# A convolution with top-1 mixture of experts on one core: the list rows of a routing unit made as an outer product of 16-bit one-hots

## The chip, the cores and the metric

The program runs on one core of a Trainium2 chip. Its metric is the device time of one execution in microseconds (us); the kernel before takes 1145.64 us, the median of three runs from 1144.6 to 1146.14 us. Engines are named as in the profile: PE multiplies matrices, PEld is its loading of weights, DVE, ACT and POOL are the vector, scalar and general engines, SP issues transfers.

## The reference

A short causal convolution comes first. Each of 8 heads has 7 taps, made into weights by a softmax; head h of token s is the weighted sum of the same 24 columns of tokens s-6 to s.

```python
x_pad = np.concatenate([np.zeros((B, pad, D)), x], axis=1)      # B 8, S 2880, D 192
x_unf = x_pad[:, idx, :].reshape(B, S, K, H, group)
x = np.einsum('hk,bskhg->bshg', w, x_unf).reshape(B * S, D)     # 23040 tokens
```

Then each token goes to one of 4 groups (largest logit of x @ w_group), and in it to one of 4 experts (largest logit of x @ w_expert[g]). Its output is the product of the two softmax values times relu(x @ w1[g, e]) @ w2[g, e], with 1024 hidden features.

```python
mask_e = e_idx == e
h = np.maximum(xg[mask_e] @ w1[g, e], 0.0)
out[tok_idx] = combined[:, None] * (h @ w2[g, e])
```

So every token needs its row, its scale, and a place in the list of its expert; the list tells the expert stage which rows to fetch.

## The kernel before

**Units.** Routing is cut into 192 blocks of 120 tokens, and these into 18 units u0 to u17: of 4, 8, 12, 8, 8 and 8 blocks, and then of 12 each. `unit(u)` (L402) is a generator that yields between its steps, so that a unit's steps are issued between those of its neighbours and, later, between the steps of the experts. A unit loads x, runs the convolution on PE (L452) and copies it on ACT into a tile xc (L461; three buffers), transposes it (L475, L483), takes the logits (L495, L497, L500), turns them back (L507, L508) and decides on DVE (L539 to L568). L568 writes the scale into xc, and L570 stores xc to a table xcd in device memory, from ACT's queue. A later unit's L461 takes the buffer again, and so waits for that store to land.

**The list rows.** ohx (bf16, block innermost) is the one-hot of the 16 experts; L557 sums it over the blocks into cum. L579 and L580 are two small matmuls on the last column of cum; from them come the running ends of the lists and the place of each token (L583 to L591). L593 and L595 split a place into one of 128 rows of its window (16 experts, 8 eighths each) and one of 32 columns. Then, in halves of `HB2` = 6 blocks, L608 compares a table of 128 numbers with the row (ohl, f16, 128 numbers a block), L615 compares a table of 32 with the column (ohr), and L619 multiplies ohr by the token's number (ohv). From u6 on (`LP`) these stand in the written order, with yields between (`HGAP`, `LG`). L624 to L626 make rowi, the table rows that the unit writes. L633 multiplies ohl by ohv, one matmul of 128 weights a block, summed over the unit's blocks: 192 in all, with 192 moving columns (the 32, six times) in u0 to u7 and 32 in the others. L640 and L642 turn the sum into token numbers (lsi), and the POOL issues a transfer (L645) that writes lsi into the table idtab.

**The table's fill.** Before any of that, two transfers (L269, L272, `clear_table`) fill idtab from SBUF. Their source, `fill`, takes a buffer of the tile ohl (L265), which has two in the pool.

**Experts.** From unit u5 on (`NEED`) the expert stage runs beside routing: lists are loaded (L1157), rows gathered (L717), turned (L750 to L767), the hidden layer is computed (L817 or L786), then back (L835, L839 or L801, L805), L898 scales the result into ys, and L888 scatters it. Loads of expert weights (L666 to L670) go through SP's queue, and DVE and ACT cast them (L683, L691, L698).

The order of each engine is fixed when the program is built: the generators say what may come next, and a planner merges the steps by their costs.

## Time and profile before

| | |
|---|---|
| median of three runs | 1145.64 us (1144.6 to 1146.14) |
| the profiled execution | 1152.26 us |
| its span, first to last instruction | 1150.4 us |
| granted clock of PE, mean | 0.977 |
| PE busy | 1072.8 us, 93% |
| PEld busy | 971.1 us, 84% |
| DVE busy | 752.4 us, 65% |
| ACT busy | 644.1 us, 56% |
| POOL busy | 523.5 us, 46% |

The first expert matmul starts 117.87 us after the first instruction; the last of the lists is written at about 445 us. Rows of the trace are in microseconds from the span's start. What stands in square brackets in a row is the time for which that engine sat idle just before, and what ended the idle time. The busy share of the whole span is a mean over stages that have different limits.

### The profile page before, as it was taken

What the parts mean: (1) busy time and instruction counts of PE and PEld (TensorE: products, weight loads), DVE (VectorE), ACT (ScalarE), POOL (GpSimd) and SP (SyncE); (2) the same over time, 40 slices, a digit from 0 to 9 for tenths busy, and PEclk for the clock granted to TensorE, in tenths of its full rate; (3) what the DMA queues carried; (4) which work ended last, traced back from release to release, by engine and by line L of the source; (5) the groups of instructions that cost most, each with busy time, mean ns of one, the idle gap of its engine ahead of it and who ended that gap; (6) DMA issues with size and microseconds to landing.
All of it is one profiled execution on the core that took longest, in us unless ns stands there. A gap on an engine that the chain in (4) does not pass through costs nothing.

```text
span 1150.4 us, 20931 instructions
## 1 busy us (share of the span) xinstructions
PE 1072.8 (93%) x7124; PEld 971.1 (84%) x7124; DVE 752.4 (65%) x1671; ACT 644.1 (56%) x1362; POOL 523.5 (46%) x611
## 2 busy tenths in 40 slices
PE   6565999998999998999999999999999999999996
PEld 4444788987989998889899999999999988989986
DVE  3465878987778756576565555655556665687874
ACT  5445657765657554454455445554545555677873
POOL 3004143333334454554545454545445554487773
PEclk9878989999999999999999999999999999999998
DMA  8767688999566432332253223322333435499970
GB/s 185 186 158 228 160 222 215 252 234 216 156 155 164 122 106 85 116 112 67 83 137 113 72 76 99 113 74 73 103 101 106 133 92 157 116 257 257 252 201 19
DMA packets 143167, 166.08 MB, mean 144 GB/s; under 512 B 18946, under 2 KB 124397, under 8 KB 143054
## 3 DMA queue, kind: packets, MB, share of 16 engines
q1 hardware_dynamic: 100974, 111.04, 36.4%
q0 software_dynamic: 18752, 35.85, 10.5%
q10 hardware_dynamic: 23328, 17.80, 6.6%
q8 instruction: 57, 0.93, 0.3%
q14 instruction: 56, 0.46, 0.1%
HBM read 129.43 MB, written 36.58 MB: 144 GB/s over the span
## 4 chain that ended last, share of the span: by engine, by line
PE 70%; DMA 5%; DVE 5%; issue 4%; ACT 3%; POOL 1%; POOLq 0%; ACTq 0%; DVEq 0%
PE ph L786 21%; PE ph L817 11%; PE pm L801 7%; PE po L801 7%; PE po L835 7%; PE pm L805 3%; PE po L805 3%; PE po L839 3%; PE pm L452 3%; DMA rawc<-in_moe_w 2%; DMA xg<-xcd,idpt 2%; DVE hl L823 1%; DVE cw L698 1%; PE ph L852 1%; PE ph L750 1%
## 5 line engine op out<-in xcount | busy, mean ns | idle before, releaser
L888 POOL DMA_INDIRECT out<-ys,idp x160 | 174.3, 1090 | 267.9 <-DVE ys L898 192.0
L791 DVE SCALAR_TENSOR_TENSOR hl<-ph,hh 128x512 fp32r<-128x512 f32 x208 | 142.2, 689 | 141.7 <-ACT hh L790 141.3
L790 ACT ACTIVATE hh<-ph 128x512 fp32r<-128x512 f32 x208 | 123.0, 600 | 170.6 <-PE ph L786 167.6
L717 POOL DMA_INDIRECT xg<-xcd,idp x160 | 175.3, 1096 | 93.8 <-issue 40.5
L835 PE MATMUL po<-cw,hh 128*128 128x384 f32 x592 | 193.2, 379 | 3.0 <-DVE ys L898 3.0
L817 PE MATMUL ph<-xa,ah 128*128 128x256 f32 x592 | 169.2, 307 | 0.0
L839 PE MATMUL po<-cw,hl 128*128 128x192 f32 x592 | 149.6, 253 | 0.0
L801 PE MATMUL po<-cw,hh 128*128 128x384 f32 x416 | 134.1, 359 | 0.0
L801 PE MATMUL pm<-cw,hh 128*128 128x384 f32 x416 | 133.9, 359 | 0.0
L823 DVE SCALAR_TENSOR_TENSOR hl<-ph,hh 128x512 fp32r<-128x512 f32 x148 | 101.1, 684 | 42.7 <-ACT hh L822 42.5
L822 ACT ACTIVATE hh<-ph 128x512 fp32r<-128x512 f32 x148 | 87.9, 596 | 62.3 <-PE ph L817 49.8
L835 PEld LDWEIGHTS po<-cw,hh 128*128 128x128 f32 x592 | 112.7, 190 | 7.6 <-DVE ys L898 3.6
L817 PEld LDWEIGHTS ph<-xa,ah 128*128 128x128 f32 x592 | 113.1, 191 | 4.4 <-issue 1.5
L839 PEld LDWEIGHTS po<-cw,hl 128*128 128x128 f32 x592 | 114.4, 193 | 2.0
L805 PE MATMUL pm<-cw,hl 128*128 128x192 f32 x416 | 104.2, 250 | 0.0
L805 PE MATMUL po<-cw,hl 128*128 128x192 f32 x416 | 104.1, 250 | 0.0
L786 PE MATMUL ph<-xa,ah 128*128 128x512 f32 x208 | 86.0, 413 | 1.4 <-DVE hl L791 1.4
L698 DVE TENSOR_TENSOR cw<-rawc,cw 128x768 fp32r<-128x768 f32 x82 | 76.0, 955 | 15.1 <-ACT cw L697 14.5
L817 PE MATMUL ph<-xb,bh 128*128 128x256 f32 x296 | 84.0, 284 | 0.7 <-DVE xb L767 0.7
L805 PEld LDWEIGHTS po<-cw,hl 128*128 128x128 f32 x416 | 79.1, 190 | 5.8
L817 PE MATMUL ph<-xb,bl 128*128 128x256 f32 x296 | 83.9, 284 | 0.0
L817 PE MATMUL ph<-xa,al 128*128 128x256 f32 x296 | 83.7, 283 | 0.0
(275 smaller groups left out, 2656.2 us busy)
## 6 DMA issues: line engine op xcount, KB each, us to landing
rawc<-in_moe_w SPq DMA_DIRECT2D x82, 384.0 KB
raw<-in_moe_w SPq DMA_DIRECT2D x41, 512.0 KB
raw<-in_moe_w SPq DMA_DIRECT2D x82, 256.0 KB
xcd<-xc ACTq DMA_DIRECT2D x13, 1085.6 KB
xin<-in_x SPq DMA_DIRECT2D x7, 1134.0 KB
xc<-in_moe_w SPq DMA_DIRECT2D x18, 384.0 KB
xin<-in_x SPq DMA_DIRECT2D x6, 1039.5 KB
xin<-in_moe_w SPq DMA_DIRECT2D x9, 512.0 KB
```

The lines of the kernel that those rows point to most:

```text
L717: nc.gpsimd.indirect_dma_start(out=xs[t][:, 0:XW], out_offset=None, in_=xcd[0:known, :], in_offset=bass.IndirectOffsetOnAxis(ap=ids[:, t, ...
L786: nc.tensor.matmul(out=hp.rearrange("p a b -> p (a b)"), lhsT=W[wgt][:, fs], rhs=xx, start=i == 0, stop=i == len(ops) - 1)
L790: nc.scalar.activation(out=hh, in_=hp, func=AF.Relu)
L791: nc.vector.scalar_tensor_tensor(out=hl, in0=hp, scalar=0.0, in1=hh.bitcast(F32), op0=ALU.max, op1=ALU.subtract,)
L801: nc.tensor.matmul(out=oo[t][:, 0:2 * D], lhsT=hh[:, ts], rhs=cw[:, f].rearrange("p a d -> p (a d)"), start=f == 0, stop=False,)
L805: nc.tensor.matmul(out=oo[t][:, 0:D], lhsT=hl[:, ts], rhs=cw[:, f, 0, :], start=False, stop=f == NF - 1,)
L817: nc.tensor.matmul(out=hp[:, j], lhsT=wgt[:, fs], rhs=xx, start=i == 0, stop=i == len(ops) - 1)
L822: nc.scalar.activation(out=hh, in_=hp, func=AF.Relu)
L823: nc.vector.scalar_tensor_tensor(out=hl, in0=hp, scalar=0.0, in1=hh.bitcast(F32), op0=ALU.max, op1=ALU.subtract,)
L835: nc.tensor.matmul(out=oo[t][:, 0:2 * D], lhsT=hh[:, j, ts], rhs=cw[:, f].rearrange("p a d -> p (a d)"), start=f == 0, stop=False,)
L839: nc.tensor.matmul(out=oo[t][:, 0:D], lhsT=hl[:, j, ts], rhs=cw[:, f, 0, :], start=False, stop=f == NF - 1,)
L888: nc.gpsimd.indirect_dma_start(out=outviews[nscat[0] % len(outviews) if view is None else view], out_offset=bass.IndirectOffsetOnAxis(ap=i ...
```

## The change

The unit's row one-hot is no longer compared number by number. posr (L596) is the column as f16, row8 (L599) is the low three bits of the row, so which eighth of the expert's window it is. oh8 (L606, L607) is the one-hot of the eighth times the token's number, and ohl (L610) is the outer product of ohx with oh8: 16 experts by 8 eighths by the blocks of the unit, block innermost, in one instruction, with all operands 16 bits wide. ohr (L617) compares a table of 32 by the blocks with posr, also block innermost. The token's number is now in ohl, and ohv is gone. ohl has one buffer in the pool instead of two, as large as a whole unit needs, and `fill` takes that one. The list matmuls (L629, L633 before) read their weights and their moving columns with a step of as many elements as the unit has blocks. One yield group (`HGAP`) stands between ohl and ohr, and the other (`LG`) is gone. The rare path's result uses a buffer of another tile; it does not run with these inputs.

```diff
--- before.py
+++ after.py
@@ -262,7 +262,7 @@
 
     LIM = SLOT * ROUNDS
     LR = LIM // LF
-    fill = pa.tile([P, HB2, P], F16, name="ohl", bufs=2).rearrange("p b q -> p (b q)").bitcast(I32)
+    fill = pa.tile([P, P * UB], F16, name="ohl").bitcast(I32)
     nc.gpsimd.memset(fill[0:LF * E, 0:LR], BIG)
 
     def clear_table():
@@ -313,17 +313,17 @@
     io = pa.tile([P, 512], F32, name="lts", bufs=2).bitcast(I32)[:, 0:N // BT]
     nc.gpsimd.iota(io[:, 0:UB], pattern=[[BT, UB]], base=1, channel_multiplier=1)
     nc.vector.tensor_copy(out=vals, in_=io[:, 0:UB])
-    assert UB * BT <= 2048
+    assert UB * BT <= 2048 and VS == 64 * LH and LE <= 64
     io3 = rt.tile([P, E * UB], F32, name="pos").bitcast(I32)
-    nc.gpsimd.iota(io3[:, 0:P], pattern=[[VS, E], [LH, LE]], base=int(RND), channel_multiplier=0)
-    iop = const.tile([P, P], F32, name="iop")
-    nc.vector.tensor_copy(out=iop, in_=io3[:, 0:P])
-    nc.gpsimd.iota(io3[:, P:P + LH], pattern=[[-1, LH]], base=0, channel_multiplier=0)
-    ior = const.tile([P, LH], F32, name="ior")
-    nc.vector.tensor_copy(out=ior, in_=io3[:, P:P + LH])
-    nc.gpsimd.iota(io3[:, P + LH:P + LH + E], pattern=[[VS, E]], base=-1, channel_multiplier=0)
+    iol = const.tile([P, LE, UB], I32, name="iol")
+    nc.gpsimd.iota(iol, pattern=[[1, LE], [0, UB]], base=0, channel_multiplier=0)
+    nc.gpsimd.iota(io3[:, 0:E], pattern=[[VS, E]], base=-1, channel_multiplier=0)
     eoff = const.tile([P, E], F32, name="eoff")
-    nc.vector.tensor_copy(out=eoff, in_=io3[:, P + LH:P + LH + E])
+    nc.vector.tensor_copy(out=eoff, in_=io3[:, 0:E])
+    io4 = rt.tile([P, LH * UB], I32, name="dd")
+    nc.gpsimd.iota(io4, pattern=[[-1, LH], [0, UB]], base=0, channel_multiplier=0)
+    ior = const.tile([P, LH, UB], F16, name="ior")
+    nc.vector.tensor_copy(out=ior, in_=io4.rearrange("p (c b) -> p c b", c=LH))
 
     sel = const.tile([P, E], F32, name="sel")
     nc.vector.tensor_reduce(
@@ -592,33 +592,30 @@
         posb = rt.tile([P, 2, UB], F32, name="posb")[:, :, 0:nb]
         nc.vector.tensor_scalar(
             out=posb[0:Q, 0], in0=pn, scalar1=-(LH - 1) / 2, scalar2=RND, op0=ALU.add, op1=ALU.add)
+        posr = rt.tile([P, UB], F16, name="posh")[:, 0:nb]
         nc.vector.scalar_tensor_tensor(
-            out=posb[0:Q, 1], in0=posb[0:Q, 0], scalar=RND, in1=pn, op0=ALU.subtract, op1=ALU.subtract)
-
-        halves = []
-        for b0 in range(0, nb, HB2):
-            n = min(HB2, nb - b0)
-            if u >= LP and b0:
-                for _ in range(HGAP):
-                    yield
-            ohl = pa.tile([P, HB2, P], F16, name="ohl", bufs=2)
-            ohr = rt.tile([P, HB2, LH], F16, name="ohr", bufs=1)
-            ohv5 = pa.tile([P, HB2, LH], F16, name="ohv", bufs=2)
-            bs = slice(b0, b0 + n)
-            hold(u >= LP, nc.vector.tensor_tensor(
-                out=ohl[0:Q, 0:n], in0=iop[0:Q].unsqueeze(1).broadcast_to([Q, n, P]), in1=bc(posb[0:Q, 0, bs], P),
-                op=ALU.is_equal,
-            ))
-            if u >= LP:
-                for _ in range(LG):
-                    yield
-            hold(u >= LP, nc.vector.tensor_tensor(
-                out=ohr[0:Q, 0:n], in0=ior[0:Q].unsqueeze(1).broadcast_to([Q, n, LH]), in1=bc(posb[0:Q, 1, bs], LH),
-                op=ALU.is_equal,
-            ))
-            hold(u >= LP, OHE.tensor_tensor(
-                out=ohv5[0:Q, 0:n], in0=ohr[0:Q, 0:n], in1=bc(vals[0:Q, bs], LH), op=ALU.mult))
-            halves.append((b0, n, ohl, ohv5))
+            out=posr[0:Q], in0=posb[0:Q, 0], scalar=RND, in1=pn, op0=ALU.subtract, op1=ALU.subtract)
+        row8 = rt.tile([P, UB], I32, name="row8")[:, 0:nb]
+        nc.vector.tensor_scalar(
+            out=row8[0:Q], in0=posb[0:Q, 0].bitcast(I32), scalar1=VS // LH - 1, scalar2=None, op0=ALU.bitwise_and)
+        oh8 = rt.tile([P, LE, UB], F16, name="oh8")[:, :, 0:nb]
+
+        def over(a, n):
+            return a.unsqueeze(1).broadcast_to([Q, n, nb])
+
+        nc.vector.tensor_tensor(out=oh8[0:Q], in0=over(row8[0:Q], LE), in1=iol[0:Q, :, 0:nb], op=ALU.is_equal)
+        nc.vector.tensor_tensor(out=oh8[0:Q], in0=oh8[0:Q], in1=over(vals[0:Q, 0:nb], LE), op=ALU.mult)
+        ohl = pa.tile([P, P * UB], F16, name="ohl")[:, 0:P * nb].rearrange("p (e l b) -> p e l b", e=E, l=LE)
+        ohr = rt.tile([P, LH * UB], F16, name="ohr")[:, 0:LH * nb].rearrange("p (c b) -> p c b", c=LH)
+        hold(u >= LP, nc.vector.tensor_tensor(
+            out=ohl[0:Q], in0=ohf[0:Q].unsqueeze(2).broadcast_to([Q, E, LE, nb]),
+            in1=oh8[0:Q].unsqueeze(1).broadcast_to([Q, E, LE, nb]), op=ALU.mult,
+        ))
+        if u >= LP:
+            for _ in range(HGAP):
+                yield
+        hold(u >= LP, nc.vector.tensor_tensor(
+            out=ohr[0:Q], in0=ior[0:Q, :, 0:nb], in1=over(posr[0:Q], LH), op=ALU.is_equal))
         rows = rt.tile([P, E + 1], F32, name="rows")
         rowi = rt.tile([P, 1], I32, name="rowi")
         nc.vector.tensor_tensor(out=rows[:, 0:E], in0=eo, in1=sel, op=ALU.mult)
@@ -628,13 +625,13 @@
             yield
         pl = bank("l")
         nrep = REPO if u < REPU else 1
-        for b0, n, ohl, ohv5 in halves:
-            for k in range(n):
-                nc.tensor.matmul(
-                    out=pl[:, 0:nrep * LH].rearrange("p (r n) -> p r n", r=nrep), lhsT=ohl[0:Q, k],
-                    rhs=ohv5[0:Q, k].unsqueeze(1).broadcast_to([Q, nrep, LH]),
-                    start=b0 + k == 0, stop=b0 + k == nb - 1,
-                )
+        for k in range(nb):
+            nc.tensor.matmul(
+                out=pl[:, 0:nrep * LH].rearrange("p (r n) -> p r n", r=nrep),
+                lhsT=ohl[0:Q, :, :, k].rearrange("p e l -> p (e l)"),
+                rhs=ohr[0:Q, :, k].unsqueeze(1).broadcast_to([Q, nrep, LH]),
+                start=k == 0, stop=k == nb - 1,
+            )
         lv5 = rt.tile([P, LH], F32, name="lv5", bufs=1)
         lsi = rt.tile([P, LH], I32, name="lsi")
         nc.vector.tensor_scalar(
@@ -882,7 +879,10 @@
     after = []
 
     def finish(oo, ids, xs, hold=False, rare=False):
-        ys = ff.tile([P, 2, D], F32, name="ysr" if rare else "ys", bufs=1 if rare else YB)
+        if rare:
+            ys = ff.tile([P, 2, SLOT], F32R, name="hl", bufs=HB).bitcast(F32)[:, :, 0:D]
+        else:
+            ys = ff.tile([P, 2, D], F32, name="ys", bufs=YB)
 
         def scatter(t, view=None):
             nc.gpsimd.indirect_dma_start(
```

The next rows are DVE's around u0's one-hots and u1's softmax, before. ohl_398 is u0's row one-hot, lsi_415 its token numbers, lg_338 are u1's logits.

```order
L595 SCALAR_TENSOR_TENSOR posb_395<-posb_395,posn_210 120x4 [waits DVE_49]
L608 TENSOR_TENSOR ohl_398<-iop_153,posb_395 120x512
L615 TENSOR_TENSOR ohr_399<-ior_156,posb_395 120x128 [waits DVE_49]
L619 TENSOR_TENSOR ohv_400<-ohr_399,vals_147 120x128 [waits DVE_49]
L640 TENSOR_SCALAR lv5_414<-pm_409 128x32 [waits PE_49]
L642 SCALAR_TENSOR_TENSOR lsi_415<-pm_409,lv5_414 128x32 [waits DVE_49]
L539 TENSOR_REDUCE mx_461<-lg_338 120x40 [waits Activation_49]
L540 TENSOR_TENSOR dd_462<-lg_338,mx_461 120x160 [waits DVE_49]
```

After, in the same place; DMAHW5 and DMAHW4 are the two transfers that fill idtab, and ohl_404 is in the buffer that they read.

```order
L599 TENSOR_SCALAR row8_399<-posb_395 120x4
L617 TENSOR_TENSOR ohr_405<-ior_159,posh_397 120x128 [waits DVE_49]
L606 TENSOR_TENSOR oh8_401<-row8_399,iol_152 120x8x4 [waits DVE_49]
L607 TENSOR_TENSOR oh8_401<-oh8_401,vals_147 120x8x4 [waits DVE_49]
L610 TENSOR_TENSOR ohl_404<-ohx_330,oh8_401 120x512 [waits DMAHW5_49,DMAHW4_49,DVE_49]
L637 TENSOR_SCALAR lv5_418<-pm_413 128x32 [waits PE_49]
L639 SCALAR_TENSOR_TENSOR lsi_419<-pm_413,lv5_418 128x32 [waits DVE_49]
L224 MEMSET xin_727 6x192 [waits DMAHW2_49,PE_49]
L539 TENSOR_REDUCE mx_465<-lg_338 120x40 [waits Activation_49]
```

The wait for the two transfers has moved in front of u0's row one-hot, and u0's lsi and u1's softmax stand behind it.

DVE's rows at u1's one-hots, before; rowi_690 is u1's, and DMASW6 is the transfer that writes u0's list, which reads the buffer that rowi_690 takes.

```order
L595 SCALAR_TENSOR_TENSOR posb_534<-posb_534,posn_210 120x8 [waits DVE_49]
L608 TENSOR_TENSOR ohl_537<-iop_153,posb_534 120x768
L615 TENSOR_TENSOR ohr_538<-ior_156,posb_534 120x192 [waits DVE_49]
L608 TENSOR_TENSOR ohl_543<-iop_153,posb_534 120x256 [waits DMAHW5_49,DMAHW4_49]
L619 TENSOR_TENSOR ohv_539<-ohr_538,vals_147 120x192 [waits DVE_49]
L626 TENSOR_TENSOR rowi_690<-rows_689,goff_165 128x1 [waits DMASW6_49]
L224 MEMSET xin_727 6x192 [waits DMAHW2_49]
L615 TENSOR_TENSOR ohr_544<-ior_156,posb_534 120x64 [waits DVE_49]
L619 TENSOR_TENSOR ohv_545<-ohr_544,vals_147 120x64 [waits DVE_49]
```

After:

```order
L623 TENSOR_TENSOR rowi_690<-rows_689,goff_165 128x1 [waits DMASW6_49,DVE_49]
L593 TENSOR_SCALAR posb_538<-posn_210 120x8 [waits DVE_49]
L596 SCALAR_TENSOR_TENSOR posh_540<-posb_538,posn_210 120x8 [waits DVE_49]
L599 TENSOR_SCALAR row8_542<-posb_538 120x8
L617 TENSOR_TENSOR ohr_548<-ior_159,posh_540 120x256 [waits DVE_49]
L606 TENSOR_TENSOR oh8_544<-row8_542,iol_152 120x8x8 [waits DVE_49]
L607 TENSOR_TENSOR oh8_544<-oh8_544,vals_147 120x8x8 [waits DVE_49]
L610 TENSOR_TENSOR ohl_547<-ohx_479,oh8_544 120x1024 [waits DVE_49]
L637 TENSOR_SCALAR lv5_565<-pm_556 128x32 [waits PE_49]
```

Before, the wait for the fill stood at the second half's ohl_543; now u1 has one row one-hot without it, and rowi's wait stands in front of all of u1's one-hots.

PE's rows at u0's list, before; pm_409 is the list's sum, the rows behind it are u2's convolution (L452) and transposes (L475), and u1's logits turned back (L507).

```order
L633 LDWEIGHTS ohl_398
L633 MATMUL pm_409<-ohv_400,ohl_398 128x192
L452 MATMUL pm_419<-xin_174,band_190 120x288
L452 MATMUL pm_431<-cw_176,band_190 120x192
L475 MATMUL pm_448<-ident_112,xc_346 128x120 [waits DVE_49,PE_49]
L475 MATMUL pm_448<-ident_112,xc_346 128x120 x3
L452 MATMUL pm_454<-cw_176,band_190 120x192 [waits Activation_49]
L507 MATMUL pm_457<-ident_112,lts_443 120x128 [waits Activation_49]
L507 MATMUL pm_457<-ident_112,lts_443 120x128
```

After:

```order
L629 LDWEIGHTS ohl_404
L629 MATMUL pm_413<-ohr_405,ohl_404 128x192
L452 MATMUL pm_423<-xin_174,band_190 120x288
L452 MATMUL pm_435<-cw_176,band_190 120x192
L475 MATMUL pm_452<-ident_112,xc_346 128x120 [waits DVE_49,PE_49]
L475 MATMUL pm_452<-ident_112,xc_346 128x120 x3
L452 MATMUL pm_458<-cw_176,band_190 120x192 [waits Activation_49]
L507 MATMUL pm_461<-ident_112,lts_447 120x128 [waits Activation_49]
L507 MATMUL pm_461<-ident_112,lts_447 120x128
```

The order is the same: what follows u0's list on PE follows it still, with the list now released by ohl_404.

DVE's rows at u7's one-hots, before, with the experts' ys (L898) among them:

```order
L595 SCALAR_TENSOR_TENSOR posb_1566<-posb_1566,posn_210 120x12 [waits DVE_49]
L608 TENSOR_TENSOR ohl_1569<-iop_153,posb_1566 120x768
L615 TENSOR_TENSOR ohr_1570<-ior_156,posb_1566 120x192 [waits DVE_49]
L898 SCALAR_TENSOR_TENSOR ys_1609<-po_1322,xg0_211,ys_1609 128x192 [waits Activation_49]
L619 TENSOR_TENSOR ohv_1571<-ohr_1570,vals_147 120x192 [waits DVE_49]
L608 TENSOR_TENSOR ohl_1598<-iop_153,posb_1566 120x768
L615 TENSOR_TENSOR ohr_1599<-ior_156,posb_1566 120x192 [waits DVE_49]
L898 SCALAR_TENSOR_TENSOR ys_1609<-po_1323,xg0_211,ys_1609 128x192 [waits Activation_49]
L619 TENSOR_TENSOR ohv_1600<-ohr_1599,vals_147 120x192 [waits DVE_49]
```

After:

```order
L596 SCALAR_TENSOR_TENSOR posh_1560<-posb_1558,posn_210 120x12 [waits DVE_49]
L599 TENSOR_SCALAR row8_1562<-posb_1558 120x12
L606 TENSOR_TENSOR oh8_1564<-row8_1562,iol_152 120x96 [waits DVE_49]
L898 SCALAR_TENSOR_TENSOR ys_1599<-po_1314,xg0_211,ys_1599 128x192 [waits Activation_49]
L607 TENSOR_TENSOR oh8_1564<-oh8_1564,vals_147 120x96 [waits DVE_49]
L610 TENSOR_TENSOR ohl_1567<-ohx_1310,oh8_1564 120x1536 [waits DVE_49]
L617 TENSOR_TENSOR ohr_1568<-ior_159,posh_1560 120x384
L898 SCALAR_TENSOR_TENSOR ys_1599<-po_1315,xg0_211,ys_1599 128x192 [waits Activation_49]
```

ys stands ahead of two of the four instructions that make the one-hots, and u7's matmuls have one release instead of two.

## Rows read from the trace of the kernel before

**Rows 1.** page: busy time of each engine; the chain that ended last

```profile
PE 1072.8 (93%) x7124; PEld 971.1 (84%) x7124; DVE 752.4 (65%) x1671; ACT 644.1 (56%) x1362; POOL 523.5 (46%) x611
...
PE 70%; DMA 5%; DVE 5%; issue 4%; ACT 3%; POOL 1%; POOLq 0%; ACTq 0%; DVEq 0%
```

**Rows 2.** stretches: length, busy us of PE, PEld, DVE, ACT, POOL, granted clock, DMA

```profile
40.00:80.00 40.00, 22.09 (x138) 17.04 (x137) 22.85 (x86) 16.02 (x43) 2.92 (x3) 0.78 0.59 152
...
120.00:160.00 40.00, 34.58 (x251) 31.14 (x250) 31.36 (x83) 21.93 (x45) 10.68 (x8) 0.91 0.71 183
...
440.00:480.00 40.00, 35.02 (x232) 32.65 (x231) 23.09 (x50) 17.53 (x37) 23.96 (x35) 0.96 0.33 95
...
480.00:520.00 40.00, 40.00 (x232) 36.10 (x232) 26.56 (x68) 19.34 (x43) 21.82 (x33) 1.00 0.31 92
```

**Rows 3.** lines by shape, DVE: total us, mean ns | idle before them, releaser

```profile
L608 DVE TENSOR_TENSOR ohl<-iop,posb 120x768 f16<-120x768 f32 x30 | 28.5, 950 | 0.0
...
L615 DVE TENSOR_TENSOR ohr<-ior,posb 120x192 f16<-120x192 f32 x30 | 10.5, 350 | 0.0
...
L619 DVE TENSOR_TENSOR ohv<-ohr,vals 120x192 f16<-120x192 f16 x30 | 10.4, 348 | 0.1
```

**Rows 4.** instructions in time (start, us, what, idle before): first one-hots

```profile
23.88 6.25 SPq L269 DMA_DIRECT2D idtab<-ohl  x1
...
26.58 0.69 DVE L608 TENSOR_TENSOR ohl<-iop,posb 120x512 f16<-120x512 f32 x1
...
37.58 0.43 DVE L608 TENSOR_TENSOR ohl<-iop,posb 120x256 f16<-120x256 f32 x1 [0.21 <-DMA idtab<-ohl]
...
46.49 0.16 DVE L626 TENSOR_TENSOR rowi<-rows,goff 128x1 int32<-128x1 f32 x1 [8.22 <-DMA idtab<-lsi,rowi]
```

**Rows 5.** instructions in time: u0's list, u1's result and its store, u2's logits

```profile
28.45 0.49 PE L633 MATMUL pm<-ohv,ohl 120*128 120x192 f16 x4
...
34.65 0.19 DVE L568 RECIPROCAL xc<-se 120x8 f32<-120x8 f32 x1
...
34.88 0.33 ACTq L570 DMA_DIRECT2D xcd<-xc  x1
...
42.05 0.33 ACT L461 ACTIVATE xc<-ph 120x192 f32<-120x192 f32 x1 [4.13 <-DMA raw<-in_moe_w]
...
49.63 0.37 ACT L508 ACTIVATE lg<-pm 120x240 f32<-120x240 f32 x1 [0.31 <-PE pm L507]
```

**Rows 6.** instructions in time: last store in front of the experts

```profile
96.60 0.32 ACTq L570 DMA_DIRECT2D xcd<-xc  x1
...
109.99 0.42 ACT L461 ACTIVATE xc<-ph 120x288 f32<-120x288 f32 x1 [8.79 <-DMA xcd<-xc]
...
117.87 0.50 PE L817 MATMUL ph<-xa,ah 128*128 128x256 f32 x1
```

**Rows 7.** PE in time and by shape: list pairs, 16 strided columns, 4-byte weights

```profile
128.74 1.16 PE L633 MATMUL pm<-ohv,ohl 120*128 120x192 f16 x12
...
309.54 0.47 PE L633 MATMUL pm<-ohv,ohl 120*128 120x32 f16 x12
...
31.21 0.57 PE L475 MATMUL pm<-ident,xc 120*128 120x120 f32 x4
...
L580 PE MATMUL pm<-cum,ones 120*128 120x16 bf16 x11 | 2.1, 191 | 0.0
```

**Rows 8.** instructions in time: the waits for DVE at 138 to 152 us

```profile
138.68 0.16 DVE L626 TENSOR_TENSOR rowi<-rows,goff 128x1 int32<-128x1 f32 x1 [2.56 <-DMA idtab<-lsi,rowi]
...
140.44 0.45 PE L835 MATMUL po<-cw,hh 128*128 128x384 f32 x1 [1.06 <-DVE ys L898]
...
151.78 1.28 PE L452 MATMUL pm<-xin,band 126*120 126x288 f32 x2 [2.76 <-DVE lsi L642]
```

**Rows 9.** instructions in time, PE: the end of routing

```profile
442.04 0.30 PE L633 MATMUL pm<-ohv,ohl 120*128 120x32 f16 x6 [1.25 <-DVE ohv L619]
...
457.19 0.33 PE L754 MATMUL pm<-ident,xg 128*128 128x128 f32 x1 [2.32 <-POOL xg L733]
```

## The prediction

> **What bounds the kernel now.** I read the page first: PE is busy for 93% of the span and holds 70% of the chain that ended last; DVE, on which the change works, has 65% and 5% [rows 1]. That says that DVE time is worth something only where PE waits for it, so the next view is the busy time in stretches of 40 us [rows 2]. In 40:80 PE is busy 22.09 us and its granted clock is 0.78; in 120:160 it lacks 5.4 us; in 440:480, where routing ends, 5.0 us; and 480:520, with no routing in it, reads 40.00 of 40.00. So there are three parts: a front until the first expert matmul at 117.87 us [rows 6], where routing waits for itself and for transfers; a middle until about 460 us, where routing runs beside the experts and PE is nearly full; and a rest that has no routing. The change touches the first two.
>
> Third, the instructions in time in the front. u0's row one-hot runs at 26.58 us; the fill of the table is issued at 23.88 us (6.25 us until the issue is through), and it has landed at 37.58 us, when u1's second one-hot, the only one that waits for it, starts. At 46.49 us DVE has idled 8.22 us for u0's list to be written, at rowi [rows 4]. Beside these stands a chain that crosses them: u1's result is ready at 34.65, its store is issued at 34.88, and ACT's next copy into that buffer, at 42.05, follows by 7.2 us. (The row names a load of weights, but by the order that copy waits for the queues of the stores.) u2's logits come off ACT at 49.63, behind it [rows 5]. The same pattern, a unit's store and then a copy that waits for its landing, repeats until u5: the store at 96.60 lets ACT on at 109.99, after 8.79 us idle, and the experts start 7.9 us later [rows 6].
>
> **The change part by part.**
>
> *The single buffer, in the front.* ohl and the source of the fill now share one buffer, so u0's outer product waits for the fill to land: it can't run at 26.6 us, but at 37.5 [rows 4]. On DVE, u1's softmax stands behind it; on PE, u2's convolution and u1's logits stand behind u0's list, which ran at 28.45 us [rows 5]. u0's list would start at about 38.2 (37.5 and 0.69 for 512 elements, as before). From list to u1's result it took 34.65 - 28.45 = 6.2 us, with PE at its full clock; after some ten idle microseconds PE may be at the lower one, as it is after its idle time in 40:80 (mean 0.78, rows 2), so I take 6.2 to 8 us: 44.4 to 46.2 us. The store then goes out about 10 to 11.5 us late. But most of that was already waited away: before, DVE stood until 46.49 us for u0's list, and ACT's next logits came at 49.63. After, the store is issued at 44.6 to 46.4. It needs between 7.2 us, as before, and 7.2 x 0.59 = 4.2 us (an estimate, by the DMA share of 0.59 in 40:80, of what is left when other loads are through; rows 2). So it lands at 48.8 to 53.6, and u2's logits follow two copies of 0.33 us behind: 49.5 to 54.3, against 49.63. This is -0.1 to 4.7 us late, and I take 2.5, a little over the middle. The wait of 8.22 us doesn't add to it: u0's list had to wait for the fill before as well and is written about 1 us later, so rowi comes at about 47.5, beside the wait for the store. From u2 to u5 each unit's store hangs on the one before it, so the 2.5 us pass on to 117.87. They would be given back only where the last landing, 13.4 us after its issue [rows 6], is set by the weight loads on the same queues. Range of this term: -1 to +5.
>
> *DVE's own work.* A unit of 12 blocks spent 2 x (950 + 350 + 348) ns = 3.3 us [rows 3]. It now has row8, two steps on 96 elements for oh8, 1536 elements of ohl and 384 of ohr. The small ones I put at 0.17, 0.25 and 0.25 us, and ohr at 0.35 to 0.55 us (192 elements take 350 ns). ohl is not shown; every row of this kind here goes by one element a cycle: 768 elements in 950 ns and 192 in 348, so 384 - 192 more cost about 0.2 us and 1536 come to 1.75 us. If two go in a cycle, it is 0.95 us. The sum is 1.9 to 3.0 us, so 0.3 to 1.4 us less in each unit; I take 0.85.
>
> The row L619 has both operands 16 bits wide and yet costs what L615 does with 32-bit input [rows 3]. The Trainium skill (VectorE: DVE Perf Modes, "What auto-detection actually checks") asks for 16 bits and a step of one in every tensor for two elements a cycle; L619 reads the token's number with a step of zero, so trace and page don't conflict, and by the page ohl takes the 0.95 us. By it the terms below would be about 1 us better together; no run so far shows it.
>
> *Where that time is worth something.* In the front the one-hots lie beside store landings: nothing. In 138.68 to 151.6 us DVE has no gap, u7's one-hots are in it, and PE waits for ys 1.06 us and for lsi 2.76 us [rows 8]. What DVE saves there comes through: 0.85 (0.3 to 1.4). ys now stands ahead of ohl, which gives part of the same wait, not more. I take -0.9. At the end of routing PE waits 1.25 us for u17's one-hots, and at 457.19 us 2.32 us for rows that are gathered through that list [rows 9]. The list now has one release, after all one-hots, instead of two; the earlier half is lost as an early start, the later half comes 0 to 1.5 us sooner. I take -1.0, with +1 to -2.6 as bounds. Elsewhere in the middle I count nothing, since I read no wait of PE for a one-hot there.
>
> *The strided matmul.* Weights and moving columns are read with a step of 12 elements of 2 bytes. Ten units (u8 to u17) have 12 pairs each, in the stretches where PE is full: 120 pairs that cost PE's time one to one. Before, 12 pairs lie in 0.47 us: (0.47 - 0.177)/11 = 27 ns a pair [rows 7]. The trace has one strided read, L580's 16 moving columns out of cum: 191 ns, where 32 columns in a row have 177; its successor starts 0.03 us behind it. That bounds the moving side at a few ns to 14 ns. For strided weights there is nothing; the nearest slow loads are of 4-byte data: four pairs of transposes in 0.57 us, (0.57 - 0.27)/3 = 100 ns a pair [rows 7], 73 ns above. So 0 to 73 ns a pair; I take 28, a doubling, as the strided moving read came to about twice the contiguous one. 120 x 28 ns = +3.4 us, between 0 and +8.8. u6 and u7 have 24 pairs of 192 columns, now 1.16 us for 12 [rows 7]; half as much again on the moving side is +1.0 us (0 to +5). The earlier units' pairs lie in waits.
>
> Two pages differ on that. By the Trainium skill (SBUF — State Buffer, "Specifications (TRN2)") a read that goes to a new line of 16 bytes at each element pays a penalty, and 24 bytes always do; by it the term is there, as the trace's strided columns suggest. By another (TensorE: Matmul & The Clock Gate, "Weight-path perf modes") the fast load of 128 weights takes them "packed or strided", and the term would be 0; that is the first rival below.
>
> *The rest.* Fewer instructions (17 of DVE) and a table of 384 made on DVE at the start, a fraction of 1 us, beside the first loads: nothing. The rare path isn't run.
>
> **The sum.** +2.5 - 0.9 - 1.0 + 3.4 + 1.0 = +5.0 us on the profiled execution: 1152.26 to 1157.3. That execution is 6.6 us above the median of the three runs, so for the median I add the same difference: 1145.64 + 5.0 = 1150.6 us.
>
> **The rivals.**
>
> *TensorE reads the strided columns at its full rate.* The place is the list pairs of the middle, the price 4.4 us. Then +2.5 - 1.9 = +0.6 remain: 1146.2 us, not slower. For it: L580's neighbours start 0.03 us apart, no more than a contiguous pair. Against it: its 14 ns. It decides from below about 12 ns a pair (144 pairs at 12 ns are 1.7 us, and with 0.6 that is the 0.2% mark).
>
> *The front gives its delay back.* The landing at 109.99 us is 13.4 us behind its store, twice what others take, so loads set it [rows 6]; if they are issued when they were, the experts start at 118 us still. Then +2.5 us: 1148.1. Against it: each store before it is late as well.
>
> *DVE's relief is worth more than I count.* Two elements a cycle give 1.4 us in every unit, and PE's missing 5.4 and 5.0 us [rows 2] shrink by 1.4 and 2.6, elsewhere in the middle by as much again as at 138 us (1.4); with free strides and the front's 2.5 it is -2.9: 1142.7 us. For it: DVE without a gap at 138 us. Against it: stretches where PE is full.
>
> *Strided weights load like 4-byte data.* +2.5 - 1.9 + 8.8 + 3 = +12.4: 1158.0 us. For it: the weights are 128 columns and the row I rest on has 16.
>
> *The outer product isn't faster*, one element a cycle: about 1 us worse than the forecast, 1151.6; it lies in the forecast's range.
>
> **How the numbers follow.** The forecast has 0.40, the strides at full rate 0.22, the front that gives back 0.14, the larger relief 0.14, the slow weights 0.10. What a measurement of this kernel can tell from no change is 0.2%, 2.3 us: 1143.3 to 1147.9. Faster: most of the larger relief (0.13), part of full rate (0.06) and of the others (0.03): 0.22. Same: 0.15 of full rate, 0.05 of the front that gives back, 0.05 of the rest: 0.25. Slower: 0.53. The likeliest case alone spans 1147 to 1155. The range from 1142 to 1157.5 leaves out half of the relief's case and somewhat more than half of the slow weights'.
>
> **What would show it.** After the change, DVE's first ohl at about 37.5 us with an idle time of some 9 us before it; u1's store at 44 to 47; L817 first at 119 to 122 us. ohl of 1536 elements at 0.95 or 1.75 us. Twelve list pairs of 32 columns at 0.47 us (full rate), 0.8 (mine) or 1.3 (slow weights). PE's wait for lsi near 152 us shorter by 0.3 to 1.4. I am wrong if the first ohl doesn't wait, if the experts start at or before 118 us, or if the pairs stay at 0.47 us.

## The result, and the profile after

The changed kernel takes 1154.82 us, the median of five runs (1153.9 to 1160.41), beside 1145.86 us for the kernel before: a ratio of 1.009 with a 95% interval of 1.0074 to 1.0107. It is slower, as forecast, but by 9.0 us where 5.0 were forecast. Its profiled execution takes 1160.41 us, with a span of 1158.7 us against 1150.4; that is 5.6 us above its median, as the profiled execution before is 6.6 above its own. On another chip the same kernel came to 1.0063 (1.0036 to 1.009), and left a second trace, of an execution of 1151.08 us.

The page of the changed kernel, the lines of [rows 1]:

```profile
PE 1098.2 (95%) x7124; PEld 983.5 (85%) x7124; DVE 734.3 (63%) x1655; ACT 644.1 (56%) x1362; POOL 518.0 (45%) x611
...
PE 77%; DMA 9%; issue 4%; DVE 4%; ACT 3%; SPq 2%; POOL 1%; POOLq 0%; DVEq 0%; ACTq 0%
```

PE is busy 25 us more and DVE 18 us less; DVE did get its relief, and PE pays. The stretches of [rows 2], after:

```profile
40.00:80.00 40.00, 33.58 (x171) 21.90 (x163) 21.23 (x91) 15.44 (x43) 2.93 (x3) 0.83 0.43 111
...
120.00:160.00 40.00, 40.00 (x265) 32.62 (x266) 29.98 (x83) 21.08 (x43) 6.97 (x6) 0.91 0.68 170
...
440.00:480.00 40.00, 36.22 (x232) 33.91 (x231) 22.40 (x54) 16.10 (x34) 21.27 (x31) 0.87 0.31 88
...
480.00:520.00 40.00, 40.00 (x232) 36.06 (x231) 25.69 (x59) 20.40 (x43) 20.29 (x29) 1.00 0.30 89
```

In 40:80 PE is busy 33.58 us, 11.5 more, in 120:160 all of the time (the waits of [rows 8] are gone), and the stretch without routing is as full as before. DVE's new one-hots by shape (after [rows 3]), and the weight loads of the lists:

```profile
L610 DVE TENSOR_TENSOR ohl<-ohx,oh 120x1536 f16<-120x1536 bf16 x13 | 12.4, 955 | 0.3
...
L617 DVE TENSOR_TENSOR ohr<-ior,posh 120x384 f16<-120x384 f16 x13 | 4.6, 352 | 0.0
...
L629 PEld LDWEIGHTS <-ohl 120*128 120x128 f16 x192 | 18.1, 153 | 33.2 <-DVE ohl L610 16.6 <-issue 14.9 <-DVE xa L753 0.6
```

1536 elements take 955 ns, where 768 took 950 before, so the rate has doubled; with row8, the two steps of oh8, and ohr (167, 253, 203 and 352 ns) a unit of 12 blocks costs DVE 1.93 us, against 3.30. A weight load of the lists went from 102 to 153 ns on average. In the front (after [rows 4, 5]):

```profile
31.19 0.42 DVE L610 TENSOR_TENSOR ohl<-ohx,oh 120x512 f16<-120x512 bf16 x1 [7.46 <-DMA idtab<-ohl]
...
40.04 0.33 ACTq L570 DMA_DIRECT2D xcd<-xc  x1
...
42.48 0.16 DVE L623 TENSOR_TENSOR rowi<-rows,goff 128x1 int32<-128x1 f32 x1 [1.49 <-DMA idtab<-lsi,rowi]
...
49.45 0.37 ACT L508 ACTIVATE lg<-pm 120x240 f32<-120x240 f32 x1 [0.26 <-PE pm L507]
...
58.11 4.32 PE L629 MATMUL pm<-ohr,ohl 120*128 120x192 f16 x12 [2.27 <-DVE ohl L610]
...
62.90 0.31 ACT L508 ACTIVATE lg<-pm 120x160 f32<-120x160 f32 x1 [6.97 <-PE pm L507]
```

u0's ohl waits 7.46 us for the fill, as predicted, but until 31.19 us and not 37.5: here the fill lands sooner. u2's logits come at 49.45 us, no later than before (49.63), and rowi's wait has shrunk from 8.22 to 1.49 us. Behind it u2's list takes 4.32 us on PE, u3's logits wait for it and come at 62.90, where they came at 60.72. At the end of the front there are u4's list on its way into the table, the load of that list by the experts (L1157), the first gather, the first turn and the first expert matmul:

```profile
90.50 0.97 POOL L642 DMA_INDIRECT idtab<-lsi,rowi  x1 [14.24 <-DMA rawc<-in_moe_w]
...
96.73 0.39 SPq L1157 DMA_DIRECT2D idp<-idtab  x1
...
103.77 1.06 POOL L714 DMA_INDIRECT xg<-xcd,idp  x1 [12.30 <-DMA xcd<-xc]
...
113.42 0.45 PE L747 MATMUL pm<-ident,xg 128*128 128x128 f32 x1 [5.61 <-DMA xg<-xcd,idp]
...
122.12 0.50 PE L814 MATMUL ph<-xa,ah 128*128 128x256 f32 x1
```

Before, and then the gather in the second trace of the changed kernel:

```profile
90.39 1.84 POOL L645 DMA_INDIRECT idtab<-lsi,rowi  x1 [18.71 <-DVE xin L224]
...
94.61 0.39 SPq L1157 DMA_DIRECT2D idp<-idtab  x1
...
97.93 1.83 POOL L717 DMA_INDIRECT xg<-xcd,idp  x1 [5.70 <-DMA idp<-idtab]
```

```profile
102.21 1.05 POOL L714 DMA_INDIRECT xg<-xcd,idp  x1 [12.61 <-DMA idp<-idtab]
```

u4's list leaves as early as before (90.50 against 90.39), and u5's store goes out at 97.02 against 96.60. The load of the list is issued 2.1 us later, and the first gather follows it by 7.0 us instead of 3.3. The row names a store there, but before and in the second trace the same wait ends with the list's load. The first turn waits for the gathers, and the experts start at 122.12 us, 4.25 later; in the second trace at 119.81. So in this pair of traces the chain of the units ends when it did before, and the delay arises in two transfers behind it. u6's list, u10's and u17's, and the stretch behind u17's (after [rows 7, 9]):

```profile
132.88 4.33 PE L629 MATMUL pm<-ohr,ohl 120*128 120x192 f16 x12
...
229.58 0.96 PE L629 MATMUL pm<-ohr,ohl 120*128 120x32 f16 x12
...
448.81 0.93 PE L629 MATMUL pm<-ohr,ohl 120*128 120x32 f16 x12 [1.59 <-DVE ohr L617]
...
450.00:452.00 2.00, 2.00 (x9) 2.00 (x9) 0.91 (x4) 0.93 (x3) 0.98 (x1) 0.50 0.00 0
```

Twelve pairs of 192 columns take 4.33 us, against 1.16; twelve of 32 take 0.96, against 0.47. At 448.81 PE has idled 1.59 us in one piece, and behind it the granted clock (the share of PE's 2.4 GHz that it is given) reads 0.50, its lower level of 1.2 GHz; in [rows 9] 1.25 us stood there, and 0.48 before the second half. In the second trace the same wait has no lower clock behind it:

```profile
444.39 0.93 PE L629 MATMUL pm<-ohr,ohl 120*128 120x32 f16 x12 [1.59 <-DVE ohr L617]
...
446.00:448.00 2.00, 2.00 (x17) 2.00 (x16) 1.06 (x4) 1.13 (x5) 0.97 (x1) 1.00 0.04 8
```

Where the 8.3 us of the span arise is read from matching matmuls of the expert stage (the same one, counted from the first, in both traces). The first is 4.25 us late; after u6's and u7's lists (at 169 us before) it is 3.5; at the end of u16 6.4; behind the end of routing (472 us) 8.9; then it grows to 10.2 at 890 us, in a stretch without routing, and the tail gives 2 back. The second trace has 1.9, 0.6, 2.0, -0.5 and 1.3 at these places, so a stage of one pair of traces is not the price of the change there. One reason is the clock. From the first expert matmul to the one at 169 us its mean is not the same before, after, in the second trace, and in the kernel before without repeats (an experiment below):

```profile
117.87:169.08 51.21, 45.79 (x345) 41.96 (x344) 42.31 (x105) 29.73 (x60) 14.79 (x10) 0.93 0.75 195
...
122.12:172.60 50.48, 50.48 (x345) 43.63 (x344) 38.60 (x100) 29.95 (x60) 11.94 (x10) 0.93 0.74 191
...
119.81:169.63 49.82, 49.82 (x345) 42.82 (x344) 38.66 (x100) 30.05 (x60) 11.92 (x10) 0.97 0.74 192
...
117.80:163.16 45.36, 41.83 (x345) 38.32 (x344) 41.00 (x104) 29.40 (x60) 17.35 (x10) 1.00 0.79 196
```

### The profile page after: what moved, and what is told of

It reads as the page before. It is cut to its first block, busy times and chain, and to the rows that moved or that the text cites. A ratio compares the mean times of both kernels' runs of the same rounds, so it can differ in the third digit from the quotient of the medians.

```text
span 1158.7 us, 20928 instructions
## 1 busy us (share of the span) xinstructions
PE 1098.2 (95%) x7124; PEld 983.5 (85%) x7124; DVE 734.3 (63%) x1655; ACT 644.1 (56%) x1362; POOL 518.0 (45%) x611
## 3 DMA queue, kind: packets, MB, share of 16 engines
q0 software_dynamic: 18752, 35.85, 10.2%
## 4 chain that ended last, share of the span: by engine, by line
PE 77%; DMA 9%; issue 4%; DVE 4%; ACT 3%; SPq 2%; POOL 1%; POOLq 0%; DVEq 0%; ACTq 0%
PE ph L783 21%; PE ph L814 12%; PE po L832 7%; PE pm L798 7%; PE po L798 7%; PE pm L452 4%; PE po L836 3%; PE pm L802 3%; PE po L802 3%; DMA xg<-xcd,idpt 3%; PE pm L629 2%; DMA rawc<-in_moe_w 2%; DMA xcd<-xc 1%; PE pm L475 1%; DMA xg<-xcd,idp 1%
## 5 line engine op out<-in xcount | busy, mean ns | idle before, releaser
L714 POOL DMA_INDIRECT xg<-xcd,idp x160 | 172.4, 1077 | 99.0 <-issue 49.1
L783 PE MATMUL ph<-xc,bh 128*128 128x512 f32 x208 | 82.9, 398 | 1.8 <-DVE hl L820 1.8
```

What stands on the lines that cost most here:

```text
L714: nc.gpsimd.indirect_dma_start(out=xs[t][:, 0:XW], out_offset=None, in_=xcd[0:known, :], in_offset=bass.IndirectOffsetOnAxis(ap=ids[:, t, ...
L783: nc.tensor.matmul(out=hp.rearrange("p a b -> p (a b)"), lhsT=W[wgt][:, fs], rhs=xx, start=i == 0, stop=i == len(ops) - 1)
```

## The experiments

Each ran five rounds beside the kernel before on the same chip; ratios are to it, with 95% intervals. On these chips the kernel before spread from 1138 to 1156 us, so differences below 0.2% are not read. The edits are shown shortened.

**Contiguous moving columns** (the changed kernel, ohr and its table ior block by block).

```diff
-ohr [.., (c b)]; in0=ior[0:Q, :, 0:nb], in1=over(posr[0:Q], LH)
+ohr [.., (b c)]; in0=ior[0:Q, 0:nb], in1=bc(posr[0:Q], LH)
-rhs=ohr[0:Q, :, k]
+rhs=ohr[0:Q, k]
```

> The changed kernel with one edit: the place one-hot ohr is stored block by block, so the list matmuls read their 32 moving columns in a row; their weights are still read with a step of 24 bytes. Theory M (the moving columns cost the time): from the profile of the changed kernel, 12 pairs of 32 columns take 0.96 us against 0.47 and 12 of 192 columns 4.33 against 1.16, which for w + 32 m and w + 192 m more a pair gives about 1.4 ns more a moving column and nothing for the weights. Then the pairs fall back to 0.47 and 1.2 us, 4.9 us come back in u8 to u17, up to 6.3 in u6 and u7 and some 2 in the front: 1142 to 1148 us. Rival W (the strided weights cost it): the pairs stay at 0.9 and 4.3 us and the time at about 1154.8 us. DVE's ohr goes by one element a cycle then, about 0.55 us instead of 0.35 for 384 elements.

1.0003 (0.9982 to 1.0024): as fast as before. Its list of u6, PE's wait for lsi behind it, and its list of u9 (PE in time):

```profile
126.35 1.21 PE L629 MATMUL pm<-ohr,ohl 120*128 120x192 f16 x12
...
148.54 1.28 PE L452 MATMUL pm<-xin,band 126*120 126x288 f32 x2 [2.56 <-DVE lsi L639]
...
195.26 0.89 PE L629 MATMUL pm<-ohr,ohl 120*128 120x32 f16 x12
```

M holds for 192 columns (1.21 us) and falls for 32: they stay at 0.89. My two equations for weights and columns took the two costs as a sum. They aren't one: weights and columns with the step take 0.96 us, weights alone 0.89, so the two reads overlap. The experts start at 115.60 us.

**The reverse: the kernel before with strided moving columns.**

```diff
-ohv5 = pa.tile([P, HB2, LH], F16, name="ohv", bufs=2)
+ohv5 = pa.tile([P, LH, UB], F16, name="ohv", bufs=2)[:, :, 0:n]
-out=ohv5[0:Q, 0:n]        rhs=ohv5[0:Q, k]
+out=ohv5[0:Q].rearrange("p c b -> p b c")        rhs=ohv5[0:Q, :, k]
```

> The kernel before with one edit: L619 writes its product so that the list matmuls read their moving columns with a step of 24 bytes; the weights are read in a row as before, and DVE's instructions, buffers and waits are the same. Theory M: 12 pairs of 32 columns take 0.95 us and 12 of 192 about 4.3, as in the changed kernel; 4.9 us more in u8 to u17, up to 6.3 in u6 and u7, where DVE's waits hide a part, and about 2 in the front: 1.006 to 1.011 of before, as slow as the changed kernel or slower, since DVE isn't relieved. Rival W (the strided weights): 0.47 and 1.2 us a list, and no change.

1.0139 (1.0106 to 1.0172), slower than the change itself and than theory M's 1.006 to 1.011. PE in time: u7's list, a late list, the first expert matmul; then DVE's L619.

```profile
152.81 4.22 PE L633 MATMUL pm<-ohv,ohl 120*128 120x192 f16 x12
...
205.55 0.88 PE L633 MATMUL pm<-ohv,ohl 120*128 120x32 f16 x12
...
123.66 0.49 PE L817 MATMUL ph<-xa,ah 128*128 128x256 f32 x1
```

```profile
L619 DVE TENSOR_TENSOR ohv<-ohr,vals 120x192 f16<-120x192 f16 x30 | 30.4, 1014 | 0.1
```

The step of the moving columns alone gives 4.22 and 0.88 us a list. The time is not its price alone, and the expectation overlooks why: DVE now writes ohv with the same step, and L619 takes 1014 ns instead of 348 [rows 3], 1.33 us more of DVE in a unit of 12 blocks. By matching matmuls the run loses 5.8 us until the first, nothing more until 169 us, and 5.0 from there to 440 us; nine or ten lists that are 0.41 us longer would be 4 of these, but DVE's share in them isn't separated.

**A buffer of its own for the fill**, alone and with contiguous columns; then, beside it, the changed kernel again; and the shared buffer put into the kernel before.

```diff
-fill = pa.tile([P, P * UB], F16, name="ohl").bitcast(I32)
+fill = ff.tile([P, 2, SLOT], F32R, name="hl", bufs=HB).rearrange("p a b -> p (a b)").bitcast(I32)
```

```diff
 the kernel before
-fill = pa.tile([P, HB2, P], F16, name="ohl", bufs=2)
+fill = pa.tile([P, 2 * HB2, P], F16, name="ohl")
+ohlu = pa.tile([P, 2 * HB2, P], F16, name="ohl")      (one a unit)
-ohl = pa.tile([P, HB2, P], F16, name="ohl", bufs=2)
+ohl = ohlu[:, b0:b0 + n]
```

> The changed kernel with one edit: the fill of the table comes from a buffer of the experts' tile hl, which is not used before 118 us, so u0's outer product doesn't wait for it. Theory B (the prediction's front term, the shared buffer): 2.5 us come back, 1152.3, and with the order that follows (the first gather waits for four stores instead of five) perhaps all 4.25 by which the experts start later: 1150.5 us. Rival S (the delay of the front comes from the strided lists of u1 to u5, 2 to 3 us each on the chain, and the wait for the fill lies beside u0's list being written): 1154 to 1155 us, no change, and the first expert matmul stays at about 122 us.

> The changed kernel with both edits: contiguous moving columns and a buffer of its own for the fill. What stays of the change is the outer product on DVE and the strided weights. Theory M with B: the gains add, and the time is below that of before, by the relief of DVE that the prediction put at 1.9 us: about 1140 to 1144 us. If the strided weights cost (W), it stays above 1150. If the wait for the fill costs nothing (S), it equals the run with contiguous moving columns alone within 1.5 us.

> The changed kernel itself, unedited, as the partner of the next one on the same chip. Both theories: 1.008 to 1.011 of before. If it comes out under 1.006, the result's ratio and the earlier run with a buffer of its own for the fill (1.0052) were not as far apart as they look.

> The changed kernel with a buffer of its own for the fill, once more, beside the unedited one. Theory B (the shared buffer delays the experts, 2.5 us by the prediction, up to 4): 0.002 to 0.0035 under the unedited one in this call. Rival S (the wait lies beside the writing of u0's list): within 0.001 of it.

> The kernel before with one edit: ohl has one buffer for a whole unit, and the fill takes it, as in the change; the comparisons, the halves and the matmuls are those of before. u0's first ohl then waits for the fill. Theory B (the prediction's front term): the experts start 2.5 us later, 1.002 of before, and up to 1.004. Rival S (the wait lies beside the writing of u0's list): u2's logits come within 1 us of 49.6 us and the time is that of before, 1.000.

Alone 1.0052 (1.0029 to 1.0074); with contiguous columns 0.9987 (0.9965 to 1.0009), 0.0016 under the run without the buffer, and not told from the kernel before, which theory M with B had it beat. Between these two, on one chip, only ohr's layout changes (on DVE it costs 0.2 us a unit): 0.0065, 7.5 us, give or take some 3. Further, on another chip, the changed kernel 1.0063 (1.0036 to 1.009) and with its own fill 1.0042 (1.0016 to 1.0067). In the kernel before the shared buffer costs: 1.0035 (1.001 to 1.006). All four have one sign, and each difference by itself lies within or near its uncertainty: about 2 us, the order of the prediction's 2.5. In that last kernel DVE waits, and yet u2's logits are not late (DVE and ACT in time), nor are the experts (115.65 us):

```profile
32.65 0.69 DVE L609 TENSOR_TENSOR ohl<-iop,posb 120x512 f16<-120x512 f32 x1 [8.54 <-DMA idtab<-ohl]
...
48.87 0.39 ACT L508 ACTIVATE lg<-pm 120x240 f32<-120x240 f32 x1
```

So where those 2 us go isn't shown by the profiles: executions differ by 2 to 4 us already in when u0's list starts. On one chip the changed kernel starts the experts at 119.81 us with the shared buffer and at 117.51 with its own, but with short lists (below) at 104.64 with the shared one and at 110.82 with its own.

**No repeats**: 32 moving columns in u0 to u7, in the changed kernel and in the one before.

```diff
-    REPO = 6
+    REPO = 1
```

> The changed kernel with one edit: the list matmuls of u0 to u7 have 32 moving columns like the others, not 192, still strided. Theory M: a pair of 32 costs 80 ns instead of 346, so u6 and u7 get 6.4 us shorter on PE and the lists in the front 2 to 3 us each: 1145 to 1149 us. Rival W (weights): a pair costs as much with 32 as with 192 apart from the columns themselves (0.3 ns each, 53 ns a pair), so 1.3 us come back in u6 and u7: about 1153 us. A third way: the 192 columns keep PE's granted clock up in the front, and without them the time falls less than by M: 1150 to 1153 us with a lower clock in 40 to 160 us.

> The kernel before with one edit: 32 moving columns in u0 to u7 instead of 192, read in a row as before. Theory M: without the step a column costs 0.3 ns, so only 24 pairs x 53 ns = 1.3 us go in u6 and u7 and little in the front: 0.998 to 1.000 of before. Rival R (the repeat is worth as much here as in the changed kernel): 0.994 to 0.996. A third way: the repeats keep PE's clock up, and without them it is slower than before, 1.001 or more.

0.9968 (0.9947 to 0.9989) and 0.9975 (0.9952 to 0.9998). The changed kernel gains about 1% and is then as fast as the kernel before with the same edit, its columns still strided; its experts start at 109.07 us, its u7's list takes 0.97 us:

```profile
136.56 0.97 PE L629 MATMUL pm<-ohr,ohl 120*128 120x32 f16 x12
```

So six times 32 columns, each read with the step, are what u0 to u7 pay for. The kernel before gains 0.25%, a little more than M had it, and its experts start at 117.80 us, no earlier.

**All three edits**, and the first and last with the fill shared.

> The changed kernel with three edits: contiguous moving columns, a buffer of its own for the fill, and 32 moving columns in u0 to u7 instead of 192. Theory M: what is left of the list matmuls is 12 pairs in about 0.5 us everywhere, so against the run with the first two edits u6 and u7 lose 0.7 us each on PE (1.21 to 0.5) and the front some tenths: 0.5 to 1.5 us below it, 0.998 to 0.999 of before less, so 0.996 to 0.998 of before. Rival R (the repeat itself, not the step, is what the run without repeats gained by, because the front's order and its transfers come out another way): 0.993 to 0.996.

> The changed kernel with contiguous moving columns and 32 of them in every unit, while the fill shares ohl's buffer. Beside the next run it prices the buffer where the lists in the front are short. Theory B: 0.002 to 0.0035 over the next run, 0.995 to 0.997 of before. Rival S: as the next run, 0.993.

> The changed kernel with contiguous moving columns, 32 of them in every unit, and a buffer of its own for the fill, once more. Both theories: 0.991 to 0.996 of before, the fastest version; this call says whether that holds against another set of runs of before.

0.9933 (0.991 to 0.9957), then 0.9953 (0.993 to 0.9976) on another chip, twice more as a partner 0.9954 and 0.9966; with the fill shared 0.996 (0.9942 to 0.9979). This version beats both kernels, by 4 to 8 us against before.

**Contiguous weights too**, in u8 to u17, in all units, and in u8 to u17 with oh8 stored block by block, each beside the three edits as partner.

```diff
+ohl [.., (b e l)] for these units
+in0=ohf .. "p e b -> p b e" .unsqueeze(3), in1=oh8 .. "p l b -> p b l" .unsqueeze(2)
-lhsT=ohl[0:Q, :, :, k]
+lhsT=ohl[0:Q, k]
```

> The changed kernel with contiguous moving columns, 32 of them in every unit, and a buffer of its own for the fill, as the partner of the next two on the same chip: 0.993 to 0.996 of before.

> The same with one edit more: in u8 to u17 the outer product is stored block by block, so the weights too are read in a row; DVE then reads oh8 with a step and one operand with a step of zero, and ohl of 1536 elements should take about 1.75 us, one element a cycle, instead of 0.955. Theory O (a pair takes as long as the slower of its two strided reads, the rest overlaps): twelve pairs go back to 0.47 us, and as PE is full there, 10 x 0.41 = 4.1 us come back: 0.0035 under the partner. Rival H (hidden): pairs at 0.47 us and the same time as the partner within 0.001. Rival D (DVE's 0.8 us more a unit delays PE): slower than the partner.

> As the last, but in all units. In the front and around u6 and u7 the one-hots are where PE waits for DVE, and ohl at one element a cycle gives 0.8 us a unit back there. Theory O with DVE on the chain in the front: 0.5 to 3 us slower than the last kernel. If DVE's rate is hidden there too, the two are the same within 0.001.

> The partner of the next one: contiguous moving columns, 32 of them in every unit, a buffer of its own for the fill; 0.993 to 0.996 of before, twelve pairs at 0.88 us.

> As e10, the weights read in a row in u8 to u17, but with oh8 stored block by block too, so that DVE reads one operand of the outer product in a row; the other still has a step of zero. If the slow 2.94 us came from the step of 24 bytes on DVE, ohl now takes about 1.75 us, one element a cycle, twelve pairs take 0.47 us, and by theory O up to 4.1 us come back, less what DVE's 0.8 us more a unit cost: 1 to 3 us under the partner, 0.997 to 0.999 of it. If the step of zero is what costs, ohl stays at 2.9 us and the time at that of e10.

Partner 0.9954 (0.9928 to 0.998), late units 0.9972 (0.9946 to 0.9998), all units 0.9999 (0.9974 to 1.0024); partner 0.9966 (0.9949 to 0.9984), oh8 by blocks 0.995 (0.9923 to 0.9977). A late list of the partner's kernel, then the late units' ohl, list and longest wait for DVE (118 to 460 us), then ohl and list with oh8 by blocks:

```profile
188.37 0.89 PE L629 MATMUL pm<-ohr,ohl 120*128 120x32 f16 x12
```

```profile
L612 DVE TENSOR_TENSOR ohl<-ohx,oh 120x1536 f16<-120x1536 bf16 x10 | 29.4, 2942 | 0.2
...
215.13 0.47 PE L636 MATMUL pm<-ohr,ohl 120*128 120x32 f16 x12
...
PE po L839 <- DVE ys L905: 5.1, 6, 1.6
```

```profile
L618 DVE TENSOR_TENSOR ohl<-ohx,oh 120x1536 f16<-120x1536 bf16 x10 | 17.5, 1753 | 0.2
...
214.63 0.47 PE L642 MATMUL pm<-ohr,ohl 120*128 120x32 f16 x12
```

With both reads in a row the lists are back at 0.47 us, so the strided weights alone hold 0.88. The time doesn't follow: DVE's one-hot goes to 2.94 us, PE waits 5.1 us for ys (1.1 in the partner's trace), and O's gain is gone. In all units the ratio is 0.0027 higher still, but not by the front, as theory O had it: the experts start at 109.74 us there and at 109.53 with the late units alone. With 1.75 us a one-hot the ratio is 0.995 beside the partner's 0.9966: a difference within the uncertainty, so that the return of 4.1 us is neither shown nor excluded.

**When the experts start.** The first expert matmul of every trace, one execution each:

| kernel | first expert matmul, us |
|---|---|
| before; without repeats; with the shared buffer; with strided columns | 117.87; 117.80; 115.65; 123.66 |
| changed, six times 32 strided columns: as it is, twice; own fill, twice | 122.12, 119.81; 120.39, 117.51 |
| changed, the columns in a row or not repeated, or both (eleven traces) | 104.64 to 115.60, median 109.07 |

Two things nearly cancel in the front. The long lists cost the changed kernel some 10 us. Without them it starts the experts some 8 us before the first three, and shorter lists alone don't do that (117.80). Which part of the change gives those 8 us, no run separates. They don't all reach the end: the version with all three edits is 4 to 8 us faster.

## Why the prediction was wrong

The direction held, and so did the two mechanisms, the shared buffer and the step of the list matmuls; a size did not. The step that failed is the price of the strided matmul, and in it the moving columns that u0 to u7 read six times: +1.0 us for u6 and u7, and for the units ahead of them "The earlier units' pairs lie in waits." I gave the lists of u1 to u5 nothing. They take 2.9 to 4.3 us each instead of 0.9 to 2.3, and they stand on the chain from a unit's one-hots to the next unit's logits. With the columns in a row 7.5 us come back (1.0052 to 0.9987), with 32 of them, across chips, about 1% (1.0063 and 1.009 to 0.9968), where the whole strided matmul was put at 4.4 us. No run shortens the lists of u1 to u5 and leaves those of u6 and u7; that the time lies in the front is read from when the experts start (117.51 to 122.12 us, and 104.64 to 115.60 with shorter lists).

That the experts start 1.9 to 4.25 us late, near the +2.5 of the prediction, is luck. The prediction has the shared buffer alone there; the runs have the long lists against a gain of the change itself, both counted as nothing.

Step by step:

- *The shared buffer, +2.5 us.* The wait is there, 7.46 us, but it ends at 31.19 us and not at 37.5, and u1's store goes out at 40.04, not at 44 to 47. Four comparisons put its price at 0.7 to 3.5 thousandths, about 2 us; about right in size, its way through the front isn't shown.
- *DVE, 0.85 us a unit less.* It was 1.37, the fast end. 1536 elements take 955 ns, as 768 did before. The page that the prediction cites agrees, with two elements a cycle for 16-bit operands with a step of one (the Trainium skill, VectorE: DVE Perf Modes, "What auto-detection actually checks"); with a step of zero in one operand the same elements took 1753 ns.
- *Its worth at 138 to 152 us, -0.9.* PE's waits there are gone, but u6's and u7's lists, 3.2 us longer each, fill the room. With the columns in a row the wait for lsi is back at 2.56 us, against 2.76 before, and with other versions it is 1.1 to 2.8: the relief of DVE isn't seen in it. The *+1.0 for u6 and u7* is 6.3 us on PE. In time the stretch is 0.7 and 1.4 us shorter than before in the two traces, but at other clocks, and the kernel before without repeats is 5.9 us shorter there at the full clock; what the term costs isn't settled.
- *The pairs of u8 to u17, 28 ns, +3.4 us.* 45 ns ((0.96 - 0.47)/11), 4.9 us on PE; with DVE's relief 2.9 and 1.5 in the time, by the two traces.
- *The end of routing, -1.0.* It was +2.5 in the one trace and -2.5 in the second, with the same wait of 1.59 us; only the first has the lower clock behind it. Other versions of the change lie between, so the term is neither shown nor refuted.
- *The reading of L580.* Its 14 ns for 16 strided columns were most of the price that was needed: it is 0.9 ns a column, 168 ns for 192 and 8 us for the 48 pairs of the front's units; 1.4 ns were measured. I carried the ratio over to a pair of 32, took half of it for 192, and didn't multiply by the columns.
- *"In the front the one-hots lie beside store landings: nothing."* With short lists the change starts the experts some 8 us earlier than before. This term, put at nothing, has the other sign and hid most of the failed one.

Of the rivals, strided weights at the rate of 4-byte data came nearest: 73 ns more a pair against 37 for weights alone. TensorE at its full rate, the outer product that isn't faster, and relief above cost fell; whether the front gives its delay back isn't told by starts at 119.81 and 122.12 us.

## What to carry to other kernels

A layout that makes one engine faster has a second reader: price that reader's step for every element it reads, repeats included, and look where the reader stands on the chain before calling it hidden. Two reads that overlap can't be told apart by undoing one of them: a list stayed at 0.88 us until both were in a row. A matmul that is repeated almost for free when its columns lie in a row is no longer so when they don't. And an edit that moves a step to one reader can give it to a writer as well: look at both before taking the time as the price of one.

## What the runs showed that was not expected

- Moving columns with a step of 24 bytes cost 1.4 ns each ((4.22 - 1.16)/(11 x 192)) beyond 0.4 in a row ((1.16 - 0.47)/(11 x 160)); u3's list, with 16 bytes, about the same (2.96 us for eight pairs, 0.95 before). With 8 bytes, in u0, it is 0.6: 0.86 us for four pairs in the run with its own fill, 0.50 with the columns in a row too, both at the full clock. The Trainium skill (SBUF — State Buffer, "Specifications (TRN2)") has the penalty for a new line at each element; the runs with 16 and 24 bytes agree and add its size. Its other page (TensorE: Matmul & The Clock Gate, "Weight-path perf modes") lets the fast load take strided weights; here twelve pairs took 0.88 us with them and 0.47 without.
- The strided list takes no longer at a lower clock. u3's and u5's lists of the changed kernel, eight pairs each with 16 bytes:

```profile
71.49:74.45 2.96, 2.96 (x10) 1.42 (x11) 0.50 (x2) 0.00 (x0) 0.00 (x0) 0.99 0.96 292
...
104.90:107.81 2.91, 2.91 (x8) 1.01 (x7) 1.21 (x3) 1.28 (x3) 2.07 (x3) 0.54 1.14 211
```

  At a mean clock of 0.99 and of 0.54 it is 2.96 and 2.91 us; in a row, before, it was 0.95 and 1.44 at 1.00 and 0.50.
- DVE pays for a step when it writes, too: 192 elements with 24 bytes between them took 1014 ns, 348 in a row.
- The 192 columns cost before too: without the repeats the kernel before is 0.25% faster.
- In 520 to 890 us, without routing, the changed kernel and its variants lose 1.2 us against the kernel before, and the kernel before with strided columns doesn't. Its cause stays open.
